# Attention's state products as 64x64 tiles in a fused retention and two-layer feed-forward kernel

## The chip, the cores and the metric

The kernel runs on one core of one Trainium2 chip. The metric is the device time of one execution in microseconds, as the median of several runs.

## The reference

Attention without softmax, with a decay: for each of 4 batches and 8 heads, 576 tokens of 64 features,

```
ret = (q @ k.T) / 8 * Dmat          # Dmat[i, j] = gamma_h ** (i - j) for i >= j, else 0
x   = ret @ v
```

The heads' results lie side by side as x, 2304 tokens by 512 features. Two layers follow:

```
xn = x / rms(x) * rms_g
y  = (silu(xn @ w_gate) * (xn @ w_val)) @ w_out      # 1536 inner features
h  = y @ w_in                                        # 2048 inner features
out = piecewise(h) @ w_out2                          # 0, (h+1)^2/4 or h
```

All of it is in fp32.

## The kernel before, in words

**Attention.** The tokens of a batch are cut into chunks of 128, four full ones (c = 0 to 3) and a short one of 64 (c = 4); with 4 batches that makes 20 chunks, numbered 0 to 19 through all batches. A running state of 64x64 a head replaces the products with earlier chunks. The heads go in four pairs u, head h of a pair in the partitions h*64 to h*64+63. `state` (line 239) holds for each pair a 128x128 block with the two heads' states on its diagonal and zeros elsewhere (line 767).

`scores` (line 412) computes a chunk's k'q products for the heads h = 0 into one PSUM bank and h = 1 into another; POOL scales q and k (`qs`, `ks`); DVE multiplies both banks by the decay into `ret`. `values` (line 439) then does the rest: for c > 0 four products of the state with qs (one 128x128 a pair, line 455), eight products of v with `ret` (a head's 64 output features by the chunk's tokens, line 459), which add up with them in the bank `x`, and for c < 4 eight products of ks with v (line 465) into a second bank, `new`. DVE adds `new` to the state (line 469; for c = 0 ACT copies it, line 471). ACT copies `x` to `xraw` (line 481) and squares it (line 482), POOL adds the squares up. A chunk that straddles a border between token blocks is copied and squared in two parts. An fp32 product is two MATMULs (passes) in the trace.

**First layer.** The tokens are in five blocks of 512 or 384 (line 30); a block goes through 12 steps of 128 inner features (`step_a`, line 580). A step has two `front` groups (gate and value, 12 MATMULs each) and the `back_a` products of the step before (12). fp32 weights and inputs are split into two fp32r parts, so each product is three fp32r ones.

**How attention lies between.** An opening, ahead of the first step, scores chunks 0 to 7 and values chunks 0 to 6; it takes its PSUM banks by turns from at0, at1 and acc0 to acc3 (line 779). The steps do the others: behind a step's first `front` one call of `values`, behind its second one of `scores`, as far as the block's goal (lines 588 and 594, `att_step` in line 487). These use the banks at0 and at1 for both: scores of heads 0 and 1, then x in at0 and `new` in at1.

**What sets the order.** Every operation is first recorded by a planner (`Plan`, line 61), which then simulates the engines with a cost for each operation (line 89) and issues in the order that comes out: on PE the earliest-recorded operation that is ready, on the others the one that is due first. It tracks PSUM by whole banks (line 84). All operations are issued from its line 135, which is why every row of the profile has that line.

The second layer comes after the first and is not touched.

Of the kernel before, what the change touches and what calls it, by code (L numbers as in the profile page):

```python
# [10 lines left out]
F32 = mybir.dt.float32  # L11
F32R = mybir.dt.float32r
U32 = mybir.dt.uint32
ACTF = mybir.ActivationFunctionType
# [4 lines left out]
B, H, S, D = 4, 8, 576, 64  # L19
NT, DM, FA, FB = B * S, H * D, 1536, 2048  # L20
P = 128
KD = DM // P
NA, NB = FA // P, FB // P
NPAIR = H // 2
NG = NPAIR // 2
CH = 128
NFULL = S // CH
# [184 lines left out]
def moe_chain_kernel(ctx: ExitStack, tc: tile.TileContext, att, tail, wa, wb, dmat, gq, gk, out):  # L212
    nc = Plan(tc.nc)
# [16 lines left out]
    ps_p = pool("ps", 1, space=PSUM)  # L230
# [205 lines left out]
            nc.vector.tensor_mul(out=ret[h][:n, :, :n], in0=ps[h][:n, :, :n], in1=d[:n, :, h, :n])  # L436
        used(2 * i)

    def values(tags):

        i = nvalued[0]
        nvalued[0] += 1
        b, c = chunks[i]
        n = tokens(i)
        at = H * D if c < NFULL else 0
        v = att_t[2 * i + 1][:n, at:at + H * D].rearrange("p (h d) -> p h d", d=D)
        ret, qs, ks = ret_t.pop(i), qs_t.pop(i, None), ks_t.pop(i, None)
        x, new = (ps_p.tile([P, 512], F32, tag=g) for g in tags)
        x = x.rearrange("p (u n) -> p u n", n=CH)
        new = new[:, :NPAIR * D].rearrange("p (u d) -> p u d", d=D)  # L450
        heads = [(u, h, slice(h * D, (h + 1) * D)) for u in range(NPAIR) for h in range(2)]

        if c:
            for u in range(NPAIR):
                nc.tensor.matmul(
                    x[:, u, :n], lhsT=state[:, u], rhs=qs[:, u], start=u == 0, stop=False, skip_group_check=True
                )
        for u, h, r in heads:
            nc.tensor.matmul(
                x[r, u, :n], lhsT=v[:, 2 * u + h], rhs=ret[h][:n, u, :n],  # L460
                start=c == 0 and u == 0, stop=True, skip_group_check=True,
            )
        if c < NFULL:
            for u, h, r in heads:
                nc.tensor.matmul(new[r, u], lhsT=ks[:, 2 * u + h], rhs=v[:, 2 * u + h], start=True, stop=True)
            for h in range(2):
                r = slice(h * D, (h + 1) * D)
                if c:
                    nc.vector.tensor_add(out=state[r, :, r], in0=state[r, :, r], in1=new[r])
                else:  # L470
                    nc.scalar.copy(out=state[r, :, r], in_=new[r])
        g0 = b * S + c * CH
        for t, s0 in enumerate(STARTS):
            lo, hi = max(g0, s0), min(g0 + n, s0 + BLOCKS[t])
            if lo < hi:
                xs, ss = x_slice(t)
                m = hi - lo
                dst = slice(lo - s0, hi - s0)
                sq = sq_p.tile([P, NPAIR, CH], F32, tag="sq", name="sq")
                src = x[:, :, lo - g0:hi - g0]  # L480
                nc.scalar.copy(out=xs[:, :, dst], in_=src)
                nc.scalar.activation(out=sq[:, :, :m], in_=src, func=ACTF.Square)
                nc.gpsimd.tensor_add(out=sq[:, :2, :m], in0=sq[:, :2, :m], in1=sq[:, 2:, :m])
                nc.gpsimd.tensor_add(out=ss[:, dst], in0=sq[:, 0, :m], in1=sq[:, 1, :m])
        used(2 * i + 1)

    def att_step(goal, what):

        tags = "at0", "at1"
        if what == "values":  # L490
            if nvalued[0] < min(goal, nscored[0]):
                values(tags)
        elif nscored[0] < min(len(chunks), goal + 1) and nscored[0] == nvalued[0]:
            scores(tags)

# [386 lines left out]
```

## Time and profile before

| | us |
|---|---|
| median of 3 runs | 924.1 |
| lowest and highest | 921.1 and 926.59 |
| the profiled execution, its own time | 922.58 |
| its span, first to last instruction | 920.5 |

In the profile a row's tiles are written output<-inputs with buffer numbers left out: `at` is at0 or at1, `at<-qs,state` a state product, `at<-ret,att` one of v with ret, `at<-att,ks` one for the new state, `at<-att` scores, `fr` a front, `acc` a back. For chunks 4 to 7 that the opening scores, the buffers `t` serve as ret, qs or ks. Two numbers with a star are the part of the array that a MATMUL uses, rows by columns.

### The profile page before, as it was taken

How to read it: one execution, taken by the hardware profiler on the slowest of the kernel's cores; microseconds unless marked ns; L12 is line 12 of the kernel's file. 1: busy time of each engine (PE TensorE's matmuls, PEld its weight loads, DVE VectorE, ACT ScalarE, POOL GpSimd, SP SyncE). 2: the span in 40 equal slices, each digit the busy share in tenths (PEclk: the TensorE clock that was granted, in tenths of full speed). 3: DMA queues.
4: the chain of work that ended last, by engine and by line, in shares of the span. 5: the costliest groups of instructions: out<-in, count | busy, mean ns of one | idle time of the engine just before them, and what ended most of it. 6: DMA issues, size and time to landing. Idle time of an engine off the chain costs nothing.

```text
span 920.5 us, 13316 instructions
## 1 busy us (share of the span) xinstructions
PE 905.2 (98%) x5098; PEld 798.2 (87%) x5098; DVE 575.6 (63%) x925; ACT 478.4 (52%) x852; POOL 70.7 (8%) x80
## 2 busy tenths in 40 slices
PE   7799999999999999999999999999999999999998
PEld 7578888888889999888899998989898998989896
DVE  3978988888888798854658545333744345434343
ACT  2447656555755655533555454545654455644443
POOL 4720100210013020100000000000000000000000
PEclk9999999999999999999999999999999999999999
DMA  9778887988859847653355387555765454756432
GB/s 362 234 265 294 293 307 255 395 301 300 313 185 396 330 141 259 257 196 104 103 178 177 104 307 264 205 172 189 268 232 194 171 193 167 266 166 213 159 137 69
DMA packets 51647, 209.94 MB, mean 228 GB/s; under 512 B 5632, under 2 KB 11392, under 8 KB 47488
## 3 DMA queue, kind: packets, MB, share of 16 engines
q1 hardware_dynamic: 45392, 199.51, 61.1%
q10 hardware_dynamic: 6192, 9.59, 2.8%
q8 instruction: 40, 0.66, 0.3%
q14 instruction: 23, 0.19, 0.1%
HBM read 167.14 MB, written 41.94 MB: 227 GB/s over the span
## 4 chain that ended last, share of the span: by engine, by line
PE 94%; DVE 3%; DMA 1%; ACT 1%; issue 1%; POOL 0%; ACTq 0%; DVEq 0%
PE fr L135 51%; PE acc L135 31%; PE at L135 12%; DMA att<-in_att_dram 1%; DVE xraw L135 1%; DVE xall L135 0%; DMA gk_sb<-in_gk_dram 0%; DVE w L135 0%; DVE t L135 0%; DVE wt L135 0%; DVE o L135 0%; DVE state L135 0%; ACT att L135 0%; ACT L135 0%; ACT sq L135 0%
## 5 line engine op out<-in xcount | busy, mean ns | idle before, releaser
L135 PE MATMUL fr<-xall,wt 128*128 128x384 f32 (+1 forms) x2424 | 512.5, 356 | 2.0 <-DVE xall L135 1.3
L135 PEld LDWEIGHTS fr<-xall,wt 128*128 128x128 f32 x2424 | 437.3, 188 | 51.9 <-DVE xall L135 2.4
L135 PE MATMUL acc<-h,wt 128*128 128x512 f32 (+1 forms) x708 | 159.4, 371 | 0.0
L135 PE MATMUL acc<-wprep,h 128*128 128x512 f32 x576 | 155.7, 394 | 0.5 <-ACT h L135 0.5
L135 PEld LDWEIGHTS acc<-h,wt 128*128 128x128 f32 x708 | 128.3, 188 | 18.3
L135 DVE TENSOR_TENSOR wt<-w,wt 128x1024 fp32r<-128x1024 f32 (+1 forms) x118 | 115.8, 993 | 25.6 <-ACT wt L135 25.1
L135 ACT CAST wt<-w 128x1024 fp32r<-128x1024 f32 (+1 forms) x118 | 96.9, 835 | 52.6 <-PE acc L135 29.6
L135 PEld LDWEIGHTS acc<-wprep,h 128*128 128x128 f32 x576 | 106.6, 188 | 15.8 <-ACT h L135 0.9
L135 DVE TENSOR_TENSOR t<-fr,t 128x512 f32<-128x512 f32 (+1 forms) x120 | 76.3, 636 | 55.7 <-PE fr L135 29.0
L135 ACT ACTIVATE att<-att 128x384 f32<-128x384 f32 x156 | 79.1, 523 | 30.8 <-DVE att L135 17.2
L135 ACT CAST h<-t 128x512 fp32r<-128x512 f32 (+1 forms) x60 | 34.6, 577 | 89.8 <-DVE t L135 89.7
L135 DVE TENSOR_TENSOR att<-fr,att 128x384 f32<-128x384 f32 x48 | 26.7, 555 | 71.0 <-ACT att L135 69.6
L135 PE MATMUL at<-wprep,h 128*128 128x512 f32 x288 | 70.3, 392 | 0.0
L135 DVE TENSOR_TENSOR h<-att,h 128x384 fp32r<-128x384 f32 x96 | 52.8, 554 | 23.5 <-ACT h L135 23.1
L135 PEld LDWEIGHTS at<-wprep,h 128*128 128x128 f32 x288 | 53.7, 188 | 10.4
L135 ACT COPY att<-fr 128x384 f32<-128x384 f32 x48 | 23.0, 479 | 75.8 <-PE fr L135 72.4
L135 ACT CAST h<-att 128x384 fp32r<-128x384 f32 x96 | 48.6, 511 | 21.3 <-DVE att L135 19.9
L135 ACT ACTIVATE t<-fr 128x512 f32<-128x512 f32 (+1 forms) x60 | 33.3, 554 | 49.5 <-PE fr L135 49.4
L135 DVE SCALAR_TENSOR_TENSOR att<-att,att 128x384 f32<-128x384 f32 x48 | 26.8, 558 | 40.9 <-ACT att L135 40.9
L135 DVE TENSOR_TENSOR h<-t,h 128x512 fp32r<-128x512 f32 (+1 forms) x60 | 38.1, 635 | 12.8 <-ACT h L135 12.6
L135 DVE SCALAR_TENSOR_TENSOR att<-att,fr 128x384 f32<-128x384 f32 x24 | 13.3, 553 | 35.8 <-ACT att L135 35.8
L135 DVE TENSOR_TENSOR xall<-xraw,xall 128x512 fp32r<-128x512 f32 (+2 forms) x32 | 26.0, 828 | 2.6 <-ACT xall L135 2.4
(141 smaller groups left out, 669.6 us busy)
## 6 DMA issues: line engine op xcount, KB each, us to landing
w<-wa SPq DMA_DIRECT2D x48, 768.0 KB, 4.6
wprep<-wod SPq DMA_DIRECT2D x48, 512.0 KB, 4.1
wt<-wfd SPq DMA_DIRECT2D x24, 1024.0 KB, 5.2
wt<-wfd SPq DMA_DIRECT2D x24, 768.0 KB, 4.4
stage<-in_wb_dram SPq DMA_DIRECT2D x32, 512.0 KB, 6.3
wfd<-wprep SPq DMA_DIRECT2D x8, 1792.0 KB, 7.3
att<-in_att_dram SPq DMA_DIRECT2D x26, 512.0 KB, 6.6
stage<-in_wa_dram SPq DMA_DIRECT2D x26, 512.0 KB, 5.3
```

The costliest lines, as they stand in the source:

```text
L135: call = lambda: getattr(real, method)(*args, **kwargs)
```

## The change

In the calls of `values` made in the steps, for 0 < c < 4, the state products become eight of 64x64, one a head. Heads of the odd pairs change sides: head h of pair u writes its output to the half (h + u) mod 2, so that four successive heads use the array's four quarters. x then lies in both banks, pairs 0 and 2 in the lower half of at0, pairs 1 and 3 in the lower half of at1, and `new` in the upper half of at0. The state is kept with the odd pairs' blocks off the diagonal, in all chunks, and x comes out with their two heads swapped; the rows of w_gate and w_val and the rms weights are permuted to match where the arguments are laid out. The calls in the opening keep their 128x128 state products, with the heads' new sides. Copies and squares of a chunk with two banks are done bank by bank.

```diff
--- before.py
+++ after.py
@@ -436,7 +436,7 @@
             nc.vector.tensor_mul(out=ret[h][:n, :, :n], in0=ps[h][:n, :, :n], in1=d[:n, :, h, :n])
         used(2 * i)
 
-    def values(tags):
+    def values(tags, four=False):
 
         i = nvalued[0]
         nvalued[0] += 1
@@ -445,30 +445,48 @@
         at = H * D if c < NFULL else 0
         v = att_t[2 * i + 1][:n, at:at + H * D].rearrange("p (h d) -> p h d", d=D)
         ret, qs, ks = ret_t.pop(i), qs_t.pop(i, None), ks_t.pop(i, None)
-        x, new = (ps_p.tile([P, 512], F32, tag=g) for g in tags)
-        x = x.rearrange("p (u n) -> p u n", n=CH)
-        new = new[:, :NPAIR * D].rearrange("p (u d) -> p u d", d=D)
-        heads = [(u, h, slice(h * D, (h + 1) * D)) for u in range(NPAIR) for h in range(2)]
-
-        if c:
+        split = four and 0 < c < NFULL
+        ps = [ps_p.tile([P, 512], F32, tag=g) for g in tags]
+        new = ps[0][:, 2 * CH:] if split else ps[1][:, :NPAIR * D]
+        new = new.rearrange("p (u d) -> p u d", d=D)
+        if split:
+            banks = [a[:, :2 * CH].rearrange("p (u n) -> p u n", n=CH) for a in ps]
+            x = [banks[u % 2][:, u // 2] for u in range(NPAIR)]
+        else:
+            banks = [ps[0].rearrange("p (u n) -> p u n", n=CH)]
+            x = [banks[0][:, u] for u in range(NPAIR)]
+
+        half = [slice(h * D, (h + 1) * D) for h in range(2)]
+        heads = [(u, h, half[h], half[(h + u) % 2]) for u in range(NPAIR) for h in range(2)]
+
+        if split:
+            for u, h, r, to in heads:
+                nc.tensor.matmul(
+                    x[u][to, :n], lhsT=state[r, u, to], rhs=qs[r, u], start=u < 2, stop=False, skip_group_check=True
+                )
+        elif c:
             for u in range(NPAIR):
                 nc.tensor.matmul(
-                    x[:, u, :n], lhsT=state[:, u], rhs=qs[:, u], start=u == 0, stop=False, skip_group_check=True
+                    x[u][:, :n], lhsT=state[:, u], rhs=qs[:, u], start=u == 0, stop=False, skip_group_check=True
                 )
-        for u, h, r in heads:
+        for u, h, r, to in heads:
             nc.tensor.matmul(
-                x[r, u, :n], lhsT=v[:, 2 * u + h], rhs=ret[h][:n, u, :n],
+                x[u][to, :n], lhsT=v[:, 2 * u + h], rhs=ret[h][:n, u, :n],
                 start=c == 0 and u == 0, stop=True, skip_group_check=True,
             )
         if c < NFULL:
-            for u, h, r in heads:
-                nc.tensor.matmul(new[r, u], lhsT=ks[:, 2 * u + h], rhs=v[:, 2 * u + h], start=True, stop=True)
-            for h in range(2):
-                r = slice(h * D, (h + 1) * D)
+            for u, h, r, to in heads:
+                nc.tensor.matmul(
+                    new[r, u], lhsT=ks[:, 2 * u + h], rhs=v[:, 2 * u + h], start=True, stop=True, skip_group_check=True
+                )
+            for h, r in enumerate(half):
+                blocks = state[r].rearrange("p (a b) (t d) -> p a (b t) d", b=2, d=D)
+                to = blocks[:, :, 1:3] if h else blocks[:, :, 0::3]
+                src = new[r].rearrange("p (a b) d -> p a b d", b=2)
                 if c:
-                    nc.vector.tensor_add(out=state[r, :, r], in0=state[r, :, r], in1=new[r])
+                    nc.vector.tensor_add(out=to, in0=to, in1=src)
                 else:
-                    nc.scalar.copy(out=state[r, :, r], in_=new[r])
+                    nc.scalar.copy(out=to, in_=src)
         g0 = b * S + c * CH
         for t, s0 in enumerate(STARTS):
             lo, hi = max(g0, s0), min(g0 + n, s0 + BLOCKS[t])
@@ -477,9 +495,10 @@
                 m = hi - lo
                 dst = slice(lo - s0, hi - s0)
                 sq = sq_p.tile([P, NPAIR, CH], F32, tag="sq", name="sq")
-                src = x[:, :, lo - g0:hi - g0]
-                nc.scalar.copy(out=xs[:, :, dst], in_=src)
-                nc.scalar.activation(out=sq[:, :, :m], in_=src, func=ACTF.Square)
+                for j, bank in enumerate(banks):
+                    src = bank[:, :, lo - g0:hi - g0]
+                    nc.scalar.copy(out=xs[:, j::len(banks), dst], in_=src)
+                    nc.scalar.activation(out=sq[:, j::len(banks), :m], in_=src, func=ACTF.Square)
                 nc.gpsimd.tensor_add(out=sq[:, :2, :m], in0=sq[:, :2, :m], in1=sq[:, 2:, :m])
                 nc.gpsimd.tensor_add(out=ss[:, dst], in0=sq[:, 0, :m], in1=sq[:, 1, :m])
         used(2 * i + 1)
@@ -489,7 +508,7 @@
         tags = "at0", "at1"
         if what == "values":
             if nvalued[0] < min(goal, nscored[0]):
-                values(tags)
+                values(tags, True)
         elif nscored[0] < min(len(chunks), goal + 1) and nscored[0] == nvalued[0]:
             scores(tags)
 
@@ -858,10 +877,15 @@
     def columns(w, n):
         return w.reshape(KD, P, n, P).transpose(2, 1, 0, 3).reshape(n, P, DM)
 
-    wa = np.concatenate([columns(moe_w_gate, NA), columns(moe_w_val, NA), moe_w_out.reshape(NA, P, DM)], axis=2)
+    def sides(a):
+
+        a = a.reshape(2, 2, 2, D, -1)
+        return np.concatenate([a[:, :1], a[:, 1:, ::-1]], axis=1).reshape(DM, -1)
+
+    wa = np.concatenate([columns(sides(moe_w_gate), NA), columns(sides(moe_w_val), NA), moe_w_out.reshape(NA, P, DM)], axis=2)
     wb = np.stack([columns(moe2_w_in, NB), moe2_w_out.reshape(NB, P, DM)])
     wb = wb.reshape(2, NPB, 2, P, DM).transpose(1, 0, 2, 3, 4)
-    rg = np.ascontiguousarray(moe_rms_g.reshape(KD, P).T)
+    rg = np.ascontiguousarray(sides(moe_rms_g).reshape(KD, P).T)
     dmat, gq, gk = _constants()
 
     nc = _bacc.Bacc("TRN2", target_bir_lowering=False, num_devices=1)
```

## Rows read from the trace of the kernel before

**Rows 1.** The page, part 1: busy time, share of the span, instructions.
```profile
PE 905.2 (98%) x5098; PEld 798.2 (87%) x5098; DVE 575.6 (63%) x925; ACT 478.4 (52%) x852; POOL 70.7 (8%) x80
```

**Rows 2.** Windows: stretch, length, busy time of each engine (instructions), clock, DMA share, GB/s.
```profile
0.00:45.00 45.00, 35.36 (x421) 29.61 (x421) 27.50 (x42) 17.39 (x32) 26.66 (x32) 0.96 0.83 297
...
60.00:165.00 105.00, 105.00 (x521) 85.18 (x519) 92.61 (x154) 64.62 (x104) 5.91 (x8) 1.00 0.85 298
```

**Rows 3.** The waits of PE from 60 to 440 us: total, times, longest.
```profile
PE fr L135 <- DVE wt L135: 0.2, 1, 0.2
```

**Rows 4.** Timeline of PE, chunk 11: start, duration, what, count, idle time before.
```profile
174.79 1.05 PE L135 MATMUL at<-qs,state 128*128 128x128 f32 x8
175.77 1.09 PE L135 MATMUL at<-ret,att 128*64 128x128 f32 x16
176.69 0.63 PE L135 MATMUL at<-att,ks 128*64 128x64 f32 x16
177.26 3.04 PE L135 MATMUL fr<-xall,wt 128*128 128x512 f32 x12
180.22 1.04 PE L135 MATMUL at<-att 64*128 64x128 f32 x13
```

**Rows 5.** Timeline of PE in windows under 0.1 us, chunks 11 and 18: single passes.
```profile
174.56 0.39 PE L135 MATMUL fr<-xall,wt 128*128 128x512 f32 x1
...
175.56 0.28 PE L135 MATMUL at<-qs,state 128*128 128x128 f32 x1
...
175.93 0.39 PE L135 MATMUL at<-ret,att 128*64 128x128 f32 x4
...
374.15 0.39 PE L135 MATMUL fr<-xall,wt 128*128 128x512 f32 x1
374.47 0.27 PE L135 MATMUL at<-att 64*64 64x64 f32 x1
```

**Rows 6.** Timeline of PE, chunk 7.
```profile
45.78 1.06 PE L135 MATMUL at<-t,state 128*128 128x128 f32 x8
48.11 0.32 PE L135 MATMUL at<-t,att 128*64 128x128 f32 x1 [1.28 <-DVE t L135]
48.13 0.33 PE L135 MATMUL at<-att,t 128*64 128x64 f32 x2
48.27 0.27 PE L135 MATMUL at<-t,att 128*64 128x128 f32 x1
```

**Rows 7.** The chain that ended last, 50 to 54 us: start, duration, what.
```profile
50.24 0.58 ACT xraw L135
...
50.82 0.50 ACT sq L135
...
54.01 2.12 PE fr L135 x8
```

**Rows 8.** Timeline of ACT, chunk 8: reads of 256 elements.
```profile
60.08 0.39 ACT L135 ACTIVATE sq<-at 128x256 f32<-128x256 f32 x1
60.34 0.66 ACT L135 COPY xraw<-at 128x256 f32<-128x256 f32 x2
```

**Rows 9.** Timeline of all engines, chunk 11: the reads behind its products.
```profile
176.91 0.59 ACT L135 COPY xraw<-at 128x512 f32<-128x512 f32 x1 [1.33 <-PE at L135]
...
177.39 0.60 ACT L135 ACTIVATE sq<-at 128x512 f32<-128x512 f32 x1
...
178.27 0.84 DVE L135 TENSOR_TENSOR state<-state,at 64x256 f32<-64x256 f32 x2
```

**Rows 10.** Timeline of PE, chunk 10: a lone product of its scores.
```profile
126.58 0.49 PE L135 MATMUL at<-att 64*128 64x128 f32 x2
127.00 0.50 PE L135 MATMUL acc<-h,wt 128*128 128x512 f32 x1
```

## The prediction

> **What bounds the kernel now.** I read the page first: TensorE (PE) is busy 98% of the span and no other engine more than 63% [rows 1]. Then the windows by stage. In the opening, up to 45 us, PE is busy for 35.4 us only; from 60 us on it has no gap at all while DVE reaches 92.6 of 105 us, ACT 64.6 and POOL 5.9 [rows 2]. The list of PE's waits, cut to 60 to 440 us, has one entry of 0.2 us [rows 3]. The reader is to see two regimes: before some 54 us the chain runs through DVE and ACT, and PE time costs nothing there; after it, each ns that attention's products take on PE is a ns of the span, and DVE, ACT and POOL matter only if they make PE wait.
>
> The change touches the state products of the chunks with 0 < c < 4 that are valued inside the steps. Of the 13 chunks valued there (7 to 19) these are 8: chunks 7, 8, 11, 12, 13, 16, 17 and 18. One of them in detail [rows 4]: four state products (eight MATMULs in the trace, for each fp32 product is two passes) start at 174.79, the sixteen passes of the products with v at 175.77, the sixteen of K'V (the new state) at 176.69, and the front goes on at 177.26. So the state part takes **0.98 us**, v's part 0.92, the new state 0.57.
>
> **The change, part by part.**
>
> *State products.* Removed: eight 128x128 passes in a row, 0.98 us with the hand-over to v's products. Added: sixteen 64x64 passes on four tiles. What a pass takes: v's products run on two column tiles, two passes at a time; the first pair takes 0.16 us (175.77 to 175.93) and the other seven (176.69 - 175.93)/7 = 0.109 us each [rows 4, 5]. Four at a time, the sixteen passes are four slots: 0.16 + 3 x 0.109 = 0.49 us. I add 0.03 for late weight loads: 0.52.
>
> *Changes of tile shape.* The full-size state products follow the front without a seam: 174.56 to 174.79 is 0.23 us, one 512-column pass [rows 4, 5]. A group of 64x64 passes comes 0.32 us after the front's last pass (374.15 to 374.47) [rows 5]: 0.09 us more. From the last state pass (175.56) to v's first is 0.21 us where a pass within the group takes 0.11 (0.77 us for seven) [rows 4, 5], so that change of shape costs 0.10; it stays, from 64x64 in place of 128x128. The new part is therefore 0.09 + 0.52 + 0.10 = 0.71 us against 0.98: **0.27 us less a chunk**. Its ends: 0.36 with a first slot as short as the others and no late loads, 0.20 with a slot's half lost to late loads.
>
> *How many count.* In chunk 7 (45.78 us) the state products lie ahead of a wait of PE of 1.28 us for DVE, and hide in it [rows 6]. Seven chunks count: 7 x 0.27 = 1.9 us (1.4 to 2.5).
>
> *Four tiles at once is nowhere in this trace.* The nearest rows show two: v's products (two column tiles, one bank) here, the scores (two row tiles, a bank each) elsewhere; each halves the time. Bounds are sixteen passes in four slots and in eight. I take four: both resources were seen shared by two, and 64x64 combines these. [...] No row here has two row tiles on one bank; the change has (rows 0 to 63 and 64 to 127 of the even pairs both write bank 0). [...]
>
> *Order of the heads.* Pairs now go left, right, right, left, in v's products of all chunks. Chunk 7 shows that PE doesn't hold program order between tiles: between the two passes of one product (48.11 and 48.27) two of a later call start (48.13) [rows 6]. The order costs nothing, then, since both tiles get the same number; cover gone, it is the fourth case.
>
> *New state in bank 0.* It moves from at1 into the upper half of at0, behind the even pairs' x. In program order it was behind v's products anyway, so nothing moves on PE, but for chunk 7, where four of its passes ran inside a wait (0.25 us at most).
>
> *ACT's reads.* x lies in two banks, so each copy and each square of 512 columns becomes two of 256: two more instructions on ACT for six chunks, four for the two that straddle a block (20 in all). Small ones follow each other after 0.26 us (60.08 to 60.34) [rows 8], large ones after 0.48 (176.91 to 177.39) [rows 9]: four small 1.04, two large 0.96, so 0.1 us more a chunk. The planner ties a read to the whole bank: the even copy now waits for the new state, 0.5 us later; behind it on ACT stand weight casts, and POOL's sum of squares waits for it. The cover is the time to the next scores, which need both banks: DVE's state update ends at 178.27 + 0.84 = 179.11, the scores start at 180.22 [rows 4, 9]. ACT, at 177.99 before, would end some 0.4 us later, still ahead of DVE. Cost 0. If the cover goes, it is the third case. The update itself keeps 64x256 elements on DVE; no DMA is added or moved on any queue, POOL's products keep their place.
>
> *Chunk 7 and the start.* Here ACT's copy and square (50.24 and 50.82) are on the chain that leads to PE's restart at 54.01 [rows 7]. The split adds 0.1; ends: 0.4 where the even copy comes late, and a gain of 1.1 if the planner sets the two reads behind the work that PE waits for. I take +0.1. The opening proper keeps its instructions; that its heads too change sides lies on PE, which has 9.6 us of idle time there [rows 2].
>
> *The planner* rewrites the order with new costs. It cuts a few groups today: a lone product of scores holds PE from 126.58 to 127.00, 0.42 us, where two passes in a group take about 0.12 [rows 4, 10]; with the 0.09 of one more entry a cut costs 0.42 - 0.12 + 0.09, about 0.4. There are six such extra pieces (three in the scores of chunk 10, one in the new state of chunk 17, two in the scores of chunk 18). All could go (-2.4), as many could come (+2.4). Taken as 0.
>
> **Sum.** -1.9 + 0.1 = -1.8 us against the profiled execution's 922.58 (span 920.5): 920.8. The median shown is 924.1, 1.5 above that execution, so the forecast against the median is **922.3 us**, 0.2% less. I call 0.5% (4.6 us) the least that a measurement here can tell from no change.
>
> **The cases.**
>
> 1. *Four at a time, nothing else moves*: 922.3, own range 920.5 to 925.5 by the ends above (2.5 + 1.1 less, or 1.4 less with 0.4 and a planner's loss of 2.4 more). Chance 0.64.
>
> 2. *Two at a time.* The sixteen passes take eight slots, 0.16 + 7 x 0.109 = 0.92; with both changes of shape 1.11 against 0.98: +0.13 a chunk, 7 x 0.13 + 0.1 = +1.0: 925.1, slower than before. It decides from 6.8 slots on (0.98 - 0.19 = 0.79 = 0.16 + 5.8 x 0.109), that is when fewer than 2.4 passes run side by side. For it: no row shows more than two. Against it: each of the two sharings was free. Chance 0.15. [...]
>
> 3. *at0 is held too long.* Bank 0 comes free only when the new state is written, copied past and added; where ACT takes a long weight cast between, the scores lose their place and are cut. Slack is 1.1 us in [rows 4, 9]; a cast can eat it. Seven cuts of 0.4: +2.8 - 1.8 = 925.1. Against it: ACT is idle for 1.33 us before that very copy [rows 9]. Chance 0.08, a quarter of it beyond 0.5%, for cuts that come in twos.
>
> 4. *Passes start in program order.* Then a head's second pass holds up the next head. The state part takes nine slots (1.22 us, +0.24 a chunk), v's products in the new order twelve in place of the eight seen (+0.44 in ten chunks, half that in the three short ones): 1.7 + 5.1 + 0.1 = +6.9: 931.0. Against it: [rows 6], and the pace of v's part before, where sixteen passes in 0.92 us are eight slots and not nine [rows 4]. [...] Chance 0.05.
>
> 5. *More is gained.* 0.36 a chunk (2.5), all six extra cuts gone (2.4), ACT's reads moved off the start's chain (1.1): 918.1. For it: each is possible. Against: all three are needed to pass 0.5%. Chance 0.08.
>
> That the change does nothing is no case: the tile shapes are written out.
>
> **How the numbers follow.** Faster by over 0.5% is case 5: 0.08. Slower is case 4 and a quarter of case 3: 0.07. Within is the rest: 0.85. The range takes in case 1's spread and cases 2 and 3, with some room for the scatter of the runs, and leaves out cases 4 and 5: 919.2 to 926.2.
>
> **What the profile after would show.** Right: state passes as 64*64 with 64x128 operands, sixteen a chunk, in 0.4 to 0.6 us, 0.32 after the front's last pass; v's part still 0.92; next scores at the same distance behind the new state, with no PE wait named after ACT or DVE; ACT with 20 instructions more, PE with 64 more. Two at a time: the sixteen take 0.9. Program order: v's part takes 1.3. Bank 0 held: scores in pieces, or a PE wait on xraw or sq. The forecast falls if the chain's restart at 54.01 moves by more than 1 us, or if the pieces of rows 10 multiply.

## The result, and the profile after

The changed kernel takes **930.69 us** as median (927.0 to 931.47) beside 923.0 us (921.1 to 926.59) for the kernel before in the same comparison: ratio 1.0072, 95% interval 1.0057 to 1.0086. The forecast was 922.3 us, with a range up to 926.2; it was wrong, and on the other side. The profiled execution of the changed kernel takes 927.2 us, its span 925.1. Its eight executions show mean granted TensorE clocks from 1.0 down to 0.993: the two at 0.998 or more take 927.0 and 927.2 us and the other six 928.28 to 931.47, so the profile shown is one of the two fastest and lacks some 3.5 us of the median's loss.

In the rows PE is TensorE, PEld its weight loads, DVE VectorE, ACT ScalarE and POOL GpSimd. The page's busy times, which answer to [rows 1], hold the predicted counts: PE 64 and ACT 20 instructions more. The windows below answer to [rows 2].

```profile
PE 908.2 (98%) x5162; PEld 796.4 (86%) x5162; DVE 570.7 (62%) x925; ACT 480.9 (52%) x872; POOL 69.0 (7%) x80
```

Windows of the changed kernel, columns as in [rows 2]:

```profile
45.00:60.00 15.00, 13.48 (x123) 10.85 (x124) 13.78 (x22) 8.72 (x14) 3.35 (x4) 0.89 0.69 228
60.00:165.00 105.00, 105.00 (x521) 85.77 (x520) 89.16 (x147) 63.87 (x106) 6.33 (x8) 1.00 0.81 281
165.00:230.00 65.00, 63.55 (x383) 51.31 (x384) 51.21 (x79) 33.80 (x57) 12.18 (x11) 1.00 0.89 328
300.00:360.00 60.00, 58.48 (x360) 54.77 (x359) 52.34 (x83) 38.75 (x65) 6.81 (x8) 1.00 0.77 298
```

Up to 165 us PE is as full as it was. New are three things: a granted clock of 0.89 between 45 and 60 us, and gaps of PE of 1.45 and 1.52 us in the two later stretches (none and 0.23 before). PE's waits from 60 to 440 us, one of 0.2 us before [rows 3], are now:

```profile
PE acc L135 <- ACT o L135: 1.4, 1, 1.4
PE at L135 <- ACT sq L135: 1.1, 1, 1.1
PE fr L135 <- ACT wt L135: 0.4, 1, 0.4
```

The two profiles don't start level: before's has a granted clock of 0.5 from 12 to 14 us and the change's has none in the opening. Chunk 7's state products start 1.7 us earlier (44.12 against 45.78), and behind them the change loses 6.3 us, not the 4.6 by which the spans differ.

The tiles themselves did what was forecast. PE's timeline at chunk 8, the counterpart of [rows 4]:

```profile
56.76 0.39 PE L135 MATMUL fr<-xall,wt 128*128 128x512 f32 x1
57.08 0.67 PE L135 MATMUL at<-qs,state 64*64 64x128 f32 x16
57.67 1.09 PE L135 MATMUL at<-ret,att 128*64 128x128 f32 x16
58.60 0.63 PE L135 MATMUL at<-att,ks 128*64 128x64 f32 x16
```

From the state products to v's it is 57.67 - 57.08 = 0.59 us in place of 0.98, the entry takes 0.32 (56.76 to 57.08) in place of 0.23, v's part still takes 0.93: 0.30 us less a chunk where 0.27 was forecast. The sixteen 64x64 passes start in four groups of four, from 57.08, 57.24, 57.35 and 57.46 us: they run four at a time.

What was not forecast stands on ACT. Its timeline at chunk 11, which answers to [rows 9]:

```profile
174.64 1.04 ACT L135 CAST wprep<-wpair 128x1024 fp32r<-128x1024 f32 x1 [3.99 <-DMA wfd<-wprep]
175.71 0.58 ACT L135 COPY o<-acc 128x512 f32<-128x512 f32 x1
...
177.87 0.70 ACT L135 ACTIVATE wpair<-stage 128x512 f32<-128x512 f32 x1
179.77 0.37 ACT L135 COPY xraw<-at 128x256 f32<-128x256 f32 x1 [1.19 <-DVE state L135]
180.04 0.39 ACT L135 ACTIVATE sq<-at 128x256 f32<-128x256 f32 x1
```

ACT's copy of the even pairs waits 1.19 us for DVE's update of the state. Before, the two read different banks and could run side by side, as they did at chunk 13 (DVE's update from 266.95 us, ACT's square from 267.18). Now both read at0, and they take turns. PE's wait of 1.45 us at this chunk is not at0's, though: the `o` for which PE waits stands on ACT behind a cast that had itself waited 3.99 us for a DMA, ahead of the chunk's reads of at0. That wait came with the redrawn order.

PE's order changed too: the planner cut the scores of chunks 9, 14 and 17 into two halves, and set chunk 17's state products in three pieces. So two theories stood against each other. **A**: bank at0 now has two readers, DVE and ACT; it comes free too late, whatever the order. **D**: the edit gains, and the redrawn order alone costs the 7 us. Two smaller rivals, **B** (the 64x64 passes cost more than they save) and **C** (the layout and the order of the heads cost), were tried at once.

### The profile page after: what moved, and what is told of

Read it like the earlier page. It is cut to its first block, busy times and chain, and to the rows that moved or that the text cites. A ratio compares the mean times of both kernels' runs of the same rounds, so it can differ in the third digit from the quotient of the medians.

```text
span 925.1 us, 13496 instructions
## 1 busy us (share of the span) xinstructions
PE 908.2 (98%) x5162; PEld 796.4 (86%) x5162; DVE 570.7 (62%) x925; ACT 480.9 (52%) x872; POOL 69.0 (7%) x80
## 4 chain that ended last, share of the span: by engine, by line
PE 92%; DMA 3%; DVE 3%; ACT 1%; issue 1%; POOL 0%; ACTq 0%; SPq 0%
PE fr L135 50%; PE acc L135 30%; PE at L135 12%; DMA wfd<-wprep 1%; DMA wt<-wfd 1%; DVE xraw L135 1%; DVE xall L135 1%; DMA att<-in_att_dram 1%; DMA gk_sb<-in_gk_dram 0%; DVE t L135 0%; DVE wt L135 0%; DVE state L135 0%; ACT wprep L135 0%; DVE w L135 0%; ACT sq L135 0%
## 5 line engine op out<-in xcount | busy, mean ns | idle before, releaser
L135 DVE TENSOR_TENSOR wt<-w,wt 128x512 fp32r<-128x512 f32 (+1 forms) x118 | 112.2, 967 | 24.6 <-ACT wt L135 24.1
L135 ACT CAST wt<-w 128x512 fp32r<-128x512 f32 (+1 forms) x118 | 96.7, 835 | 55.0 <-PE acc L135 27.9
L135 DVE TENSOR_TENSOR h<-t,h 128x512 fp32r<-128x512 f32 (+1 forms) x60 | 40.1, 668 | 12.2 <-ACT h L135 11.9
```

What stands on the lines that cost most here:

```text
L135: call = lambda: getattr(real, method)(*args, **kwargs)
```

## The experiments

All ratios are to the kernel before in the same comparison; its medians there were 922.8 to 924.5 us. The last column gives the stretches between 45 and 440 us in which the profile's granted clock, in windows of 2 us, was under 0.95. It is of one execution each, which need not be the median one: full_first's took 931.07 us and full_staged_whole's 927.33, full_staged's 925.32.

| kernel | us | ratio, 95% interval | clock below 0.95 at, us |
|---|---|---|---|
| the change | 930.69 | 1.0072 [1.0057, 1.0086] | 48-52 |
| sides | 923.98 | 0.9994 [0.9982, 1.0006] | none |
| banks | 928.98 | 1.0050 [1.0029, 1.0072] | none |
| noadd | 929.26 | 1.0058 [1.0038, 1.0077] | 50-54, 326-330 |
| early | 936.91 | 1.0132 [1.0113, 1.0151] | 60-64, 318-324 |
| old_order | 962.27 | 1.0410 [1.0385, 1.0436] | four, the longest 12 us |
| whole | 945.92 | 1.0238 [1.0214, 1.0262] | four, the longest 8 us |
| new_order | 933.92 | 1.0111 [1.0088, 1.0135] | 312-318 |
| costlier | 930.10 | 1.0062 [1.0038, 1.0087] | 52-64, 330-334 |
| full_after | 931.06 | 1.0070 [1.0052, 1.0088] | 46-52, 330-336 |
| full_first | 928.49 | 1.0048 [1.0032, 1.0064] | 48-54, 332-336 |
| reads_first | 928.74 | 1.0055 [1.0037, 1.0072] | 50-54 |
| full_whole | 928.37 | 1.0047 [1.0028, 1.0066] | 326-334 |
| full_noadd | 926.41 | 1.0033 [1.0015, 1.0050] | 48-54 |
| full_staged | 927.39 | 1.0032 [1.0017, 1.0047] | 48-54 |
| staged | 927.54 | 1.0044 [1.0027, 1.0061] | 48-54 |
| full_staged_whole | 924.28 | 1.0001 [0.9984, 1.0019] | 48-52 |
| six_whole | 923.39 | 1.0016 [0.9998, 1.0034] | none |
| before_whole | 921.66 | 0.9989 [0.9980, 0.9998] | none |

### One part at a time, the planner free

**sides** keeps only the heads' new sides and the permuted weights:

```diff
-                values(tags, True)
+                values(tags)
```

> The new layout alone: the odd pairs' heads on the other side everywhere, all state products 128x128, x in one bank. Its program has the same order on PE as the kernel before. Theory A (bank 0 is held: DVE's state update and ACT's reads of x now share a bank and follow each other, so the scores find it late): no loss, 923 us within 1.5. Theory B (the 64x64 passes themselves cost, in the tiles or in what follows them): also 923. Theory C (the new order of the heads or the swapped layout costs): 927 to 931.

**banks** has the change's banks and reads with full-size state products:

```diff
-            for u, h, r, to in heads:
+            for u in range(NPAIR):
                 nc.tensor.matmul(
-                    x[u][to, :n], lhsT=state[r, u, to], rhs=qs[r, u], ...
+                    x[u][:, :n], lhsT=state[:, u], rhs=qs[:, u], ...
```

> The change with its state products as four of 128x128 again; x still in two banks, the new state still in at0, the reads still bank by bank. Theory A (bank 0 held): the loss stays and the tiles' gain goes, so 930.7 + 7 x 0.29 = 932 to 933 us, with the scores in halves. Theory B (the 64x64 passes cost): 923 to 925. Theory D (the planner's order is a lottery in which any change of costs wins or loses some us): anywhere from 925 to 935.

**noadd** leaves out DVE's update of the state in the split chunks, so the state stays what it was there:

```diff
-                if c:
+                if split:
+                    pass
+                elif c:
```

> The change without DVE's update of the state in the eight chunks with 0 < c < 4 that the steps value (that part of the computation is left out). Theory A (bank 0 held): ACT's reads follow the new state's products at once, the bank comes free about 0.9 us sooner, and the time falls to 921 to 925 us. Theory B (64x64 passes) and theory D (lottery): no reason to fall; 928 to 932 by B, anywhere by D.

**early** squares from the SBUF copy, so that ACT leaves both banks sooner:

```diff
-                    nc.scalar.activation(out=sq[:, j::len(banks), :m], in_=src, func=ACTF.Square)
+                nc.scalar.activation(out=sq[:, :, :m], in_=xs[:, :, dst], func=ACTF.Square)
```

> The change with the squares taken from the copy in SBUF instead of from PSUM, one square for all four pairs: each bank has one read less, and ACT one instruction less a chunk. Theory A (bank 0 held): bank 0 is free some 0.4 us sooner and part of the loss goes: 924 to 929 us. Theory B: 930 to 931. Theory D: anywhere from 923 to 933, and not ordered by how long the bank is held.

C falls: sides stands at 0.9994. B falls as the cause of the whole, since banks without a tile is still 0.5% slower and the tiles take 0.6 us; what follows the tiles at chunk 7 comes below. But A foretold 932 to 933 for banks, 921 to 925 for noadd and 924 to 929 for early, and all three missed. Each of these kernels also got an order of its own from the planner, so none compares the edit alone.

### The order by itself

In the next four PE's order is a written list or comes from another cost. The lists name PE's operations by their place in the recording; the planner may issue only the next one:

```diff
             for e, q in queue.items():
+                if e == "tensor":
+                    q = [i for i in q if i == turns[-1]]
                 if not q:
                     continue
```

**old_order** is the change with PE in before's order, **new_order** the kernel before with PE in the changed kernel's order, **whole** is old_order with the pieces of four cut groups put together. **costlier** is the kernel before with one number of the planner changed:

```diff
-            return 4 * max(n, 64) / 2.4 * (0.55 if m == 64 else 1) + 5
+            return 4 * max(n, 64) / 2.4 * (0.55 if m == 64 else 1.12 if n == 128 else 1) + 5
```

> The changed kernel (64x64 tiles, x's even pairs and the new state's sums in bank at0, reads per bank), with TensorE's order pinned to that of the kernel before; the other engines are still planned. Theory A (the shared bank at0 comes free too late, because ScalarE's copy has to wait for VectorE's update): the scores behind each chunk find at0 still held whatever the order, 0.4 to 1 us in each of some seven chunks: 926 to 931 us, with waits of TensorE on ScalarE's square or copy in the chain. Theory D (the planner's new order of TensorE's groups costs the time, the edit itself gains 0.29 us in each undisturbed split chunk): 921 to 923.5 us, no wait of TensorE over 0.3 us between 60 and 440 us.

> The kernel before (128x128 state products, x in at0, new sums in at1) with TensorE's order pinned to that which the planner gave the changed kernel. Theory A: no bank is shared by x and the new sums, so nothing is held late: 922.5 to 925.5 us. Theory D: the cut score groups (0.8 us each, four of them) and the two waits behind chunks 11 and 17 (2.4 us each) come with the order: 926 to 931 us.

> The changed kernel with TensorE's order pinned to that of before, but with the cut groups of chunks 10 and 17 made whole: the four state products in two pieces, the eight score products in four pieces (1, 1, 2, 4) and in three (3, 1, 4), the eight new-state products in two (7, 1), each put where its last piece stood. Theory D: the lone score products took about 0.42 us each and a whole group of eight 0.89 us, so 1 to 3 us less than the pinned order with its cuts: 918.5 to 922 us. Theory A: the scores are held up by bank at0 as in every other chunk, so no better than the pinned order by more than 0.5 us.

> The kernel before with one number of the planner changed: a 128x128 product in fp32 is costed 12 per cent higher. The instructions, banks and tiles are those of before; only the order of issue differs. Theory A has no reason for another time: 922.5 to 925.5 us. Theory D: the order alone moves the time by more than the 0.3 per cent of a repeat; this order has no lone score products and two cut groups of six scores and two, so it may well be the faster one: 919 to 922 us, or, if it runs into waits, 926 to 930 us.

Both theories missed, though costlier, at 930.10, only just: D had 926 to 930 as its worse case. The order alone moves the time more than either allowed: costlier has before's very instructions and loses 0.6%, new_order loses 1.1% with no bank shared. And old_order loses 4.1%, where D had foretold a gain; whole stands 16 us below it, which neither foretold. PE's timeline of old_order behind chunk 17, and DVE's:

```profile
360.34 1.65 PE L161 MATMUL at<-att 64*128 64x128 f32 x6 [9.06 <-ACT sq L161]
```

```profile
356.95 1.88 DVE L161 TENSOR_TENSOR xall<-xraw,xall 128x512 fp32r<-128x512 f32 x3
358.75 0.84 DVE L161 TENSOR_TENSOR state<-state,at 64x256 f32<-64x256 f32 x2
```

The scores of chunk 18 wait 9.06 us. ACT's last read of at0 had to wait for DVE's update at 358.75, which stood in DVE's queue behind the next block's `xraw` and `xall`. That is A's mechanism, but the planner had reordered ACT and DVE around PE's list, so the size is not the change's.

### Every engine's order held

So the lists were given to all five queues: each added tile or read stands where the operation that it replaces stood, and only what a dependence forces is moved. **full_after** is the change in before's order. **reads_first** (planner free) and **full_first** (order held) record DVE's update behind ACT's reads:

```diff
+        def update():
             for h, r in enumerate(half):
...
+        if c < NFULL and not split:
+            update()
         g0 = b * S + c * CH
...
+        if split:
+            update()
```

**full_whole** is full_first with two cut groups of before's order made whole; they are chunk 9's state products (two pieces) and chunk 10's scores (four), which the expectation calls by one chunk's name.

> The changed kernel with the order of every engine pinned to that of the kernel before: the added tiles and reads stand where the one they replace stood, and only what a dependence forces is moved (VectorE's state updates up to where ScalarE's copies of x stand, chunk 7's products behind its values). Theory D (the planner's redrawn order costs the 7 us, the tiles gain 0.29 us a chunk): 920.5 to 922.5 us. Theory A (bank at0 held by two readers in turn costs, in any order): ScalarE's copies wait for VectorE's update and the scores for ScalarE: 925 to 931 us, with TensorE waits on ScalarE's copy or square.

> As the kernel with every engine's order pinned to before's, with ScalarE's reads of x recorded ahead of VectorE's state update, so that each keeps the place in its queue that it had before and VectorE's update, not ScalarE's copy, is the last reader of bank at0. Theory A: ScalarE no longer waits for VectorE, so it should come 1 to 4 us below the kernel pinned with the update first: 920 to 924 us. Theory D: 920.5 to 922.5 us, and equal to that kernel within 1 us.

> The changed kernel with one step moved: in the split chunks ScalarE's reads of x are recorded ahead of VectorE's update of the state; the planner orders as it likes. Theory A: ScalarE's copies lose their waits for VectorE (4.4 and 3.9 us in all in the changed kernel), the time falls by 2 to 6 us: 924 to 928 us. Theory D: another order is drawn, in which the scores of chunk 17 are still cut and the state products in pieces: 925 to 934 us, and the direction is not foretold.

> As the pinned kernel with the reads first, and chunk 10's four state products in one group in place of two and its eight scores in one in place of four (1, 1, 2, 4), each where its last piece stood. Both theories: a lone score product takes 0.42 us where eight take 0.89, so 0.5 to 1.5 us less than that kernel: 919 to 922 us if it stands at 920.5 to 922.5; if it does not gain, the place of the pieces was not free.

With before's order the change still takes 931.06 us: D falls as the sole cause, and A foretold this (925 to 931). Recording the reads first gains 2.6 us by the medians at a fixed order (full_first). That is within the 1 to 4 that A asked for, but the intervals overlap and 928.49 is far above its 920 to 924; with the planner free (reads_first) the interval overlaps the change's. The whole groups of full_whole gain nothing in time. The orders of these traces now match, and the places can be read. PE's timeline of the kernel before, behind chunks 16 and 17, and DVE's at its update for chunk 17:

```profile
297.99 1.16 PE L135 MATMUL at<-att 64*128 64x128 f32 x16
...
326.72 0.93 PE L135 MATMUL at<-att 64*128 64x128 f32 x6
327.86 4.10 PE L135 MATMUL fr<-xall,wt 128*128 128x384 f32 x22 [0.20 <-DVE wt L135]
```

```profile
344.36 0.85 DVE L135 TENSOR_TENSOR state<-state,at 64x256 f32<-64x256 f32 x2
```

With `new` in at1, DVE's update for chunk 17 could come 18 us behind the scores that start in at0 at 326.72. With `new` in at0 it must come ahead of them.

full_first at chunk 16, DVE's timeline and PE's:

```profile
299.26 0.85 DVE L237 TENSOR_TENSOR state<-state,at 64x256 f32<-64x256 f32 x2 [2.20 <-ACT sq L237]
```

```profile
300.56 1.16 PE L237 MATMUL at<-att 64*128 64x128 f32 x16 [0.89 <-ACT sq L237]
```

full_first at chunk 17, timeline of all engines:

```profile
330.55 0.84 DVE L237 TENSOR_TENSOR state<-state,at 64x256 f32<-64x256 f32 x2
...
331.49 0.90 PE L237 MATMUL at<-att 64*128 64x128 f32 x6 [2.12 <-ACT wt L237]
```

full_after at chunk 17, timelines of DVE, ACT and PE:

```profile
324.43 2.30 DVE L237 TENSOR_TENSOR wprep<-wpair,wprep 128x1024 fp32r<-128x1024 f32 x1
326.65 0.84 DVE L237 TENSOR_TENSOR state<-state,at 64x256 f32<-64x256 f32 x2
```

```profile
323.94 0.51 ACT L237 CAST h<-t 128x384 fp32r<-128x384 f32 x1 [0.46 <-DVE t L237]
327.58 0.65 ACT L237 COPY xraw<-at 128x256 f32<-128x256 f32 x2 [3.13 <-DVE state L237]
328.12 1.58 ACT L237 CAST wt<-w 128x1024 fp32r<-128x1024 f32 x2
```

```profile
329.23 0.61 PE L237 MATMUL fr<-xall,wt 128*128 128x384 f32 x2 [2.21 <-ACT wt L237]
...
331.55 5.45 PE L237 MATMUL fr<-xall,wt 128*128 128x384 f32 x22
```

Read full_after from the top: DVE's update stands behind a 2.30 us `wprep`; ACT's copy waits for it for 3.13 us; behind that copy in ACT's queue stand two weight casts; the front waits 2.21 us for one of them. Behind this wait the granted clock is 0.50 from 332 to 334 us, and the next 22 passes take 5.45 us in place of 4.10. Whoever reads at0 second, the other engine's queue is in its way. With the reads first it is DVE that waits at chunk 16 (2.20 us), and at chunk 17 its update ends at 331.39, 0.1 us ahead of the scores, which have waited 2.12 us; the ACT cast that the row names had ended at 330.99. At chunk 16 it is ACT's own last square that the scores wait for, of a chunk whose reads are now eight in place of four.

### Taking the second reader away

**full_noadd** is full_first without DVE's update in the split chunks. **full_staged** is whole: ACT copies the sums to SBUF behind its reads of x, and DVE adds from there, so both banks have ACT as their only reader. **staged** is the same with the planner free, **full_staged_whole** has the two groups whole.

```diff
...
         if split:
-            update()
+            held = held_p.tile([P, NPAIR, D], F32, tag="held", name="held")
+            nc.scalar.copy(out=held, in_=new)
+            update(held)
```

> The kernel with all engines pinned to before's order, ScalarE's reads first, and VectorE's update of the state left out in the split chunks (so the state is not computed). Theory A: with the second reader of at0 gone the scores behind chunks 16 and 17 find the bank free, the waits of 0.9 and 2.1 us and the low clock behind the second go, and the tiles' 0.29 us in each of six to eight chunks shows: 920.5 to 923 us. Theory D, or any other cost of the tiles: as the pinned kernel with the update, 927 to 930 us.

> All engines pinned to before's order, and ScalarE copies the state's sums to SBUF behind its reads of x (one more 128x256 copy, about 0.4 us, in each split chunk); VectorE adds from there, so that at0 and at1 have ScalarE as their only reader. The computation is whole. Theory A: no wait of ScalarE or of the scores on VectorE's update; 921 to 924.5 us. Theory D: 927 to 930 us, as the pinned kernel in which VectorE reads the bank.

> The same staging of the state's sums through ScalarE, with the planner free to order. It now keeps before's pieces of chunk 9 or 10 and cuts three other score groups in two (0.8 us each). Theory A: the held bank is gone, 922 to 927 us. Theory D: another order is drawn, 926 to 932 us.

> The pinned and staged kernel, with the four state products of the one chunk that before computed in two pieces, and its eight scores in four (1, 1, 2, 4), made whole. That saved 1.7 us of TensorE in the pinned kernel's trace (0.64, 0.64 and 0.45 at three steps). Theory A: 919.5 to 923 us, below before. Theory D: 927 to 930 us.

At the same order the ratio goes from 1.0070 with DVE's update as first reader to 1.0033 and 1.0032 without it on the bank: 0.37%, 3.4 us, with intervals that don't meet. From full_first, with DVE as second reader, it is 0.15% with intervals that overlap, so the times alone show it only for the two steps together. The traces show it chunk by chunk. From the start of a chunk's state products to the start of the next scores, in us:

| chunk | 8 | 11 | 12 | 13 | 16 | 17 | 18 |
|---|---|---|---|---|---|---|---|
| before | 5.44 | 5.43 | 5.43 | 4.75 | 4.75 | 5.56 | 5.43 |
| full_after | 5.46 | 5.05 | 5.05 | 4.39 | 5.62 | 7.23 | 5.05 |
| full_first | 5.05 | 5.05 | 5.05 | 4.40 | 5.36 | 7.95 | 5.05 |
| full_noadd | 5.05 | 5.05 | 5.05 | 4.39 | 4.72 | 5.75 | 5.04 |
| full_staged | 5.04 | 5.05 | 5.05 | 4.39 | 4.99 | 5.74 | 5.05 |
| six_whole | 5.96 | 5.04 | 5.05 | 4.40 | 4.99 | 5.56 | 5.04 |

Chunks 11, 12, 13 and 18 keep the tiles' gain (0.36 to 0.39, less the 0.09 of the longer entry ahead of it) whoever reads at0. Chunks 16 and 17 lose 0.6 to 2.4 us with DVE on the bank, and at most 0.24 without it. PE's timeline of full_staged behind chunk 17 has the waits on ACT gone:

```profile
329.03 0.93 PE L238 MATMUL at<-att 64*128 64x128 f32 x6
330.43 4.11 PE L238 MATMUL fr<-xall,wt 128*128 128x384 f32 x22 [0.46 <-DVE wt L238]
```

So A holds for about half of the loss. But full_noadd and full_staged stay some 3 us above what A foretold, and staged, at 927.54, lies above A's range and in D's; something else costs as well. full_staged_whole comes out level with before (A: 919.5 to 923), though its two whole groups alone should gain.

### Chunk 7

The first table has more of it. Of the 13 kernels with tiles in chunk 7, 11 show a low clock between 46 and 54 us in their profile; the seven without them don't (in costlier, whose order differs there, it comes at 52, behind a PE wait of 2.12 us). In windows of 2 us, the change (first fence) and banks (second), columns as in [rows 2]:

```profile
46.00:48.00 2.00, 1.48 (x21) 1.24 (x23) 2.00 (x4) 0.47 (x1) 0.97 (x1) 0.95 0.68 174
48.00:50.00 2.00, 2.00 (x19) 1.69 (x16) 1.78 (x3) 1.97 (x3) 0.40 (x1) 0.50 0.73 219
50.00:52.00 2.00, 2.00 (x8) 1.59 (x7) 1.92 (x2) 2.00 (x6) 0.27 (x1) 0.70 0.99 385
```

```profile
46.00:48.00 2.00, 1.12 (x9) 0.89 (x8) 1.97 (x4) 0.00 (x0) 0.39 (x1) 1.00 0.77 246
48.00:50.00 2.00, 1.46 (x28) 1.22 (x30) 2.00 (x4) 0.44 (x1) 0.45 (x1) 1.00 0.63 133
50.00:52.00 2.00, 2.00 (x20) 1.63 (x17) 1.64 (x4) 1.97 (x3) 1.03 (x1) 1.00 0.98 217
```

PE's timeline of the change at chunk 7, beside [rows 6]:

```profile
44.12 0.67 PE L135 MATMUL at<-t,state 64*64 64x128 f32 x16
46.35 0.43 PE L135 MATMUL at<-t,att 128*64 128x128 f32 x2 [1.56 <-DVE t L135]
46.95 1.00 PE L135 MATMUL at<-t,att 128*64 128x128 f32 x13 [0.16 <-DVE t L135]
...
48.95 3.83 PE L135 MATMUL fr<-xall,wt 128*128 128x512 f32 x11
...
54.13 3.02 PE L135 MATMUL fr<-xall,wt 128*128 128x512 f32 x12
```

DVE's `t` comes 2.2 us behind the start of the state products, 2.3 before. The shorter state products only lengthen PE's wait, from 1.28 to 1.56 us, and behind it the granted clock falls from 1.00 to 0.50; eleven front passes take 3.83 us there, twelve behind it 3.02. Estimated from the windows above, (1 - 0.50) x 2 + (1 - 0.70) x 2 = 1.6 us of work at full clock are lost. From the state products to the front behind the next scores it is 54.13 - 44.12 = 10.0 us, against 54.01 - 45.78 = 8.2 before [rows 6, 7].

In full_whole, with the same tiles and a PE wait of 1.54 us, the granted clock stays at 1.00 from 44 to 58 us:

```profile
44.31 0.67 PE L237 MATMUL at<-t,state 64*64 64x128 f32 x16
...
52.66 3.03 PE L237 MATMUL fr<-xall,wt 128*128 128x512 f32 x12 [0.16 <-DVE t L237]
```

That is 8.35 us, 0.1 more than before: the loss at chunk 7 is the low clock, and without it the prediction's +0.1 holds.

Last, **six_whole** (full_staged_whole with chunks 7 and 17 left as before) and **before_whole** (the kernel before in its own order, with the two groups whole and nothing else changed):

```diff
-        split = four and 0 < c < NFULL
+        split = four and 0 < c < NFULL and i not in (7, 17)
```

> Every engine pinned to before's order, chunk 9's state products and chunk 10's scores made whole, state's sums staged through ScalarE, and tiles of 64x64 in six of the eight chunks only: chunks 7 and 17 stay as they were in the kernel before. If the loss is the low clock behind chunk 7's wait (about 1.5 us) and at0 held behind chunk 17 (about 0.9 us), these are gone, no stretch at a granted clock of 0.5 stands between 45 and 60 us, and of the gains six times 0.3 and 1.7 us remain: 919.5 to 921.5 us on a chip where the kernel before takes 923.5. If the tiles cost elsewhere: 923 us or more.

> The kernel before with its own order, except chunk 9's state products in one group in place of two and chunk 10's scores in one in place of four; no tile, no layout changed. It should gain the 1.7 us that the step-by-step comparison shows at those groups: 921 to 922.5 us where the kernel before takes 923.5; the kernel with tiles in six chunks stands 1 to 2.5 us below it if the tiles gain what their passes say, and not below it if they do not.

six_whole's profile has no low clock anywhere before 440 us, as both chunks' causes required; its windows at chunk 7:

```profile
48.00:50.00 2.00, 2.00 (x26) 1.76 (x23) 1.63 (x4) 1.98 (x3) 1.40 (x1) 1.00 0.86 240
50.00:52.00 2.00, 2.00 (x16) 1.45 (x16) 1.03 (x2) 1.97 (x4) 1.79 (x2) 1.00 0.85 237
```

Its time did not follow: 923.39 us where 919.5 to 921.5 was expected, and 923 or more if the tiles cost elsewhere. By the medians it is 1.7 us slower than before_whole, with which it was compared on one chip. Part of it stands on ACT. The timeline of all engines in six_whole, behind chunk 8:

```profile
61.24 0.52 ACT L237 ACTIVATE sq<-at 128x128 f32<-128x128 f32 x2
...
61.65 0.84 PE L237 MATMUL at<-att 64*64 64x64 f32 x16 [0.84 <-ACT sq L237]
```

Chunks 8 and 16 straddle a block border, so their reads of x are eight in place of four, with one copy more for the staging. The scores wait 0.84 and 0.53 us for the last square, and both chunks lose (5.96 against 5.44 us, 4.99 against 4.75) where the tiles should gain. In full_staged chunk 8's state products start at 58.51 us, behind the low clock of 48 to 54 us, against 55.69 in six_whole (61.65 - 5.96), and the scores don't wait there. Between the fronts that stand at 54 and 539 us in before, six_whole's profile gains 0.4 us on it and before_whole's loses 0.8, so the tiles are ahead by 1.2 of the 1.8 us that six chunks should give; in the second layer it then loses 1.4 us, part of it in a wait of 0.6 us for a buffer filled by ACT, which before_whole does not show. Such a loss stands in full_after and full_first too (2.4 us) and not in the change's own profile. Why is left open. before_whole is the only version faster than the kernel before, by 0.1% (1 us of the 1.7 expected), and it has no tile.

## Why the prediction was wrong

- **State products and changes of tile shape: right.** 0.30 us a chunk where 0.27 was forecast; the entry at 0.32 came out as read from the rows, and the 0.03 for late weight loads, which no row or run shows, did not come (0.59 is 0.49 + 0.10).
- **Four tiles at once: right**, so case 2 falls. The first two heads write bank at0 from different row tiles into different partitions, and the sixteen passes take 0.59 us with the hand-over, where eight slots would take 0.92 + 0.10. At chunk 8 the first four of them start within 0.02 us.
- **Order of the heads: right**, cost 0 (sides at 0.9994), so case 4 falls.
- **"ACT's reads ... Cost 0": the step that failed.** It saw that the even copy waits for the new state, and measured the cover at chunk 11. It did not see that DVE and ACT, which had a bank each, now share one and that the planner ties any two engines' accesses to a bank together, reads among them: the update and the reads run one behind the other, each behind whatever else stands in the other's queue. At chunk 11 the cover sufficed; at chunks 16 and 17 it did not (0.9 to 1.2 us, and 2.2 us with 1.35 us of low clock behind it). In a fixed order this is 3.4 us of the 7. The doubled reads are not free either where a chunk straddles a block: without DVE on the bank PE still waits for ACT's square, 0.25 us at chunk 16 in full_noadd, and with the staging copy added 0.53 there and 0.84 at chunk 8 in six_whole. The planner keeps DVE and ACT apart on at0 in every kernel here, so no run shows the two on it at once. Case 3 had the place, and its two signs came (scores in pieces, a PE wait on `sq`), but it priced it as seven cuts and not as waits, and gave it 0.08.
- **"Hide in it", chunk 7: failed.** The state products do end inside a wait, but the wait then grows from 1.28 to 1.56 us and PE's granted clock falls to 0.50 behind it: +1.8 us between [rows 6] and [rows 7] in place of +0.1, of which the low clock is nearly all, as full_whole shows.
- **"The planner ... Taken as 0": right as a net, far too narrow as a bound.** The planner's order (1.0072) and before's (1.0070) serve the change alike. But the bound of 2.4 us came from counting cut groups, and an order alone moved the time by 6 (costlier) and 10 us (new_order), mostly through waits and low clock (costlier: 0.50 in the windows from 54 to 64 us; new_order: a PE wait of 3.8 us, and 0.74, 0.50 and 0.91 from 312 to 318). The count itself was one short: chunk 9's state products stand in two pieces as well.

Not closed: the 3 us by which full_staged still stands above before. Its profile places them: of 2.7 us more span, 1.4 come at chunk 7, 1.0 between the fronts at 54 and 539 us, 0.2 in the second layer. In the middle stretch the tiles should give 2.1 us, but PE's waits from 60 to 440 us, 0.2 us before [rows 3], are 2.5:

```profile
PE acc L238 <- ACT o L238: 0.9, 1, 0.9
PE fr L238 <- DVE wt L238: 0.7, 2, 0.5
PE at L238 <- ACT sq L238: 0.5, 1, 0.5
PE acc L238 <- DVE h L238: 0.4, 1, 0.4
```

The largest stands in before_whole too (0.6 us), which has no tile; why ACT's `o` comes late there is open. That the tiles' 0.3 us a chunk reach the next scores is shown for four chunks; that they reach the end of the kernel is not shown by any time.

## What to carry to other kernels

When a result moves into another PSUM bank, list who reads that bank before and after: here two engines that read a bank each ran side by side (before, chunk 13, from 266.95 and 267.18 us), and two that shared one, which this planner keeps apart, ran in turn, and each then waited for whatever stood in the other's queue (ACT 1.19 us at chunk 11 in the change, 3.13 at chunk 17 in full_after). Check the cover at every chunk: it sufficed at chunk 11 and not at 16 and 17. Making work shorter ahead of a wait gained nothing at chunk 7 and mostly cost: PE's wait grew from 1.28 to 1.56 us in the change, and in 11 of 13 profiles a granted clock of 0.50 to 0.54, in the lowest window of 2 us, followed. And where a planner sets the order, hold the order of all engines when an edit is measured, since a new order by itself was worth some 1%.

## What the runs showed of the hardware

Sixteen 64x64 passes on four tiles, two row tiles writing one bank in different partitions, started within 0.40 us at chunk 8 of the change (0.67 less one pass of 0.27), in the four slots that were forecast. TensorE's granted clock fell from 1.00 to 0.50 behind PE waits of 1.56 us (the change, chunk 7) and 2.21 us (full_after, chunk 17): the windows of 2 us show 0.95, 0.50 and 0.70 from 46 us on and 0.77, 0.50 and 0.88 from 330 us on, or, estimated from these, some 3.4 us at 0.50 each time. In one kernel (full_whole) it stayed up behind the same state products in chunk 7 (1.54 us), it stayed up in the kernel before behind 1.28 us, in the change behind 1.45 us at chunk 11, and one of the change's eight executions has a mean clock of 1.0, so no such fall; what decides between them is not known from these runs.
